# A last expert of at most 64 rows, computed on unsplit fp32 values in two column tiles

## The chip, the cores and the metric

The kernel runs on one core of a Trainium2 chip. The metric is device microseconds of one execution. Three executions of the kernel before took 591.93, 593.94 and 595.46 us (median 593.94). A fourth, taken by the hardware profiler, took 592.76 us; its trace spans 591.0 us.

## The reference

Linear attention gives the rows `x`, and a layer of eight experts works on them, each row by the one expert that its gate picks:

```python
q_s = softmax(q, axis=-1); k_s = softmax(k, axis=2)      # q, k, v: 8 x 8 x 576 x 64
x = q_s @ (k_s.T @ v)                                    # as 4608 rows of 512
logits = x @ w_gate; expert_idx = argmax(logits, axis=1)
gate_w = softmax(logits)[arange(N), expert_idx]
for e in range(8):                                       # w1[e]: 512 x 1024, w2[e]: 1024 x 512
    h = maximum(x_sorted[lo:hi] @ w1[e], 0.0)
    y_sorted[lo:hi] = h @ w2[e]
return gate_w[:, None] * y_sorted[inv_perm]
```

How many rows each expert gets is known only once the gates are computed. For the inputs of this case the reference gives 1150, 0, 542, 34, 595, 578, 0 and 1709 rows to experts 0 to 7.

## The kernel before

The first part (to about 148 us) is the attention. It writes each row of `x`, with its gate and its row number, into a scratch area in DRAM (`xs`) at a place of its expert. Then `tables` counts the rows of each expert, and `t5`, a chain of tiny VectorE operations on 8 partitions, works out a table `tab`: which experts have rows, in which order they come (expert 0, then by falling count), in how many steps, and how many tiles of 128 rows each step has. The chain ends in a matmul (`t6`) that brings the fields onto one partition, and `t8` writes them to `tab`, from which every engine reads registers.

The second part (`experts`) is a loop of steps. Each engine has its own program (`pe`, `act`, `dve`, `pool`, `sp`) and they meet at semaphores only. ACT, DVE and POOL run one `body` per step (14 here), PE one `pe_expert` per expert. A step works on up to three tiles, `W` = 384 rows. Its products are made from split values: every fp32 number is kept as a rounded high part and the low rest (`XH`, `XL`, `W1H`, `W1L`, `HH`, `HL`, `W2H`, `W2L`), and each product is three matmuls (high by high, low by high, high by low).

- `layer1(w)` on PE makes the hidden values transposed: for each of 8 blocks of 128 hidden units, 12 matmuls (3 products by 4 blocks of the inner dimension) with `w` columns. From block 5 on it waits until DVE has read an earlier block out of the same PSUM bank (`sHL[PREV[f]]`).
- ACT (`relus`) applies relu to each block into `HH`, DVE (`lows`) makes `HL` from it. In the first step of an expert ACT and DVE also split `w2` into `W2H` and `W2L`.
- `layer2(u)` makes one tile's output: 24 matmuls of 512 columns into `PY[u]`.
- ACT (`yout`) scales a tile by its gate into `YT[u]`, and POOL (`send`) scatters its rows to `out` by an indirect DMA; rows that pad a tile carry a row number out of bounds and are skipped.
- For the step that comes next, DVE (`flip`) turns the loaded rows `XB` into `XX`, ACT and DVE split that into `XH`/`XL`, and, where the next step begins another expert, they split `RAW1` (its `w1`) into `W1H`/`W1L`. SP loads rows two steps ahead (`bload`) and weights one expert ahead (`wload`).

On PE a step of one or two tiles goes through `pe_small`: `layer1` with 256 columns, then one tile, and a second one where the table says so. The last expert here has 34 rows, so its one step is `layer1(256)` and one `layer2`. Which steps ran can be counted in the trace: the 39 evictions `yt<-py` are 9 + 14 + 5 + 5 + 5 + 1 tiles.

What a step costs on PE is set by no planner: the order is that of the code, and the other engines run beside PE as the semaphores let them.

Of the kernel before, what the change touches and what calls it, by code (L numbers as in the profile page):

```python
# [16 lines left out]
P = 128  # L17
# [40 lines left out]
Q = 32  # L58
PE, DVE, ACTE, POOL, SP = "pe", "dve", "act", "pool", "sp"
# [41 lines left out]
def attention_moe(ctx: ExitStack, tc: tile.TileContext, q, k, v, w_gate, w1, w2, xs, out):  # L101
# [661 lines left out]
    def tables():  # L763
# [3 lines left out]
        base, start, steps, total, cnt, tiles, threes, rank, own = [  # L767
            small(name, [E, 1]) for name in ("base", "start", "steps", "total", "cnt", "tiles", "threes", "rank", "mykey")]
# [29 lines left out]
        MADE = 35  # L798

        def t5(sem):  # L800
# [41 lines left out]
            op('F2', 'at end on', lambda: STT(part(fld, 2), at, end, on, op0=ALU.is_equal, op1=ALU.mult))  # L842
            op('V1', 'steps', lambda: TS(V[:, 1:2], steps, 0.0, None, op0=ALU.is_gt))
# [5 lines left out]
            op('total', 'every', lambda: RED(total, every, op=ALU.add, axis=AX.X))  # L849
# [105 lines left out]
def experts(nc, tc, g):  # L955
# [21 lines left out]
    sSp, sSp2 = sem("ssp"), sem("ssp2")  # L977
    sH1, sW1, sW2 = [sem(x, NQ) for x in ("sh1", "sw1", "sw2")]
# [25 lines left out]
    def pe():  # L1004
# [71 lines left out]
        n, i = x.reg("n", 0), x.reg("i", 0)  # L1076

        def again(name, done=1):
            if done:
                x.add("it", 1)  # L1080
            x.add("n", 1)
            e.br_lt(n, E, "pe_expert", name)
            at(name)
            e.br("pe_done")

        e.br("pe_expert")
        with nc.body("pe_expert", valid_engines=[e.engine]):
# [5 lines left out]
            small = x.get(SMALL, r, 0, 2)  # L1093
# [17 lines left out]
            at("pe_small")  # L1111
            step(2 * P, 1)
# [21 lines left out]
    def act():  # L1134
# [30 lines left out]

        def body(j):
            kind = x.get(KD, j, 0, 3)
# [37 lines left out]
    def dve():  # L1205
# [24 lines left out]

        def body(j):
            fresh = x.get(LW, j, 0, 1)
# [39 lines left out]
        e.memset(g.EP[:, :, 1], 0.0).then_inc(sB, 1)  # L1272
        v = lambda t: t.rearrange("p c (u t) -> p u c t", t=P)
# [6 lines left out]
    def pool():  # L1280
# [16 lines left out]

        def body(j):
            kind = x.get(KD, j, 0, 3)
            e.drain()  # L1300
            hold(sGS, it)
# [20 lines left out]
    def sp():  # L1322
# [6 lines left out]
        def xload(j):  # L1329
            n = x.get(KD, j, 0, 3)  # L1330
# [7 lines left out]
        def bload(j):  # L1338
            n = x.get(KD, j, 0, 3)
# [87 lines left out]
```

## Time and profile before

| | |
|---|---|
| three executions | 591.93, 593.94, 595.46 us |
| the profiled execution | 592.76 us |
| its span, first to last instruction | 591.0 us |
| PE busy | 561.2 us, 95% of the span |
| DVE, ACT, POOL busy | 327.9, 254.4, 149.2 us |
| PE in the steps, 200 to 550 us | busy in all of it but 0.14 us |
| last step's first matmul, last matmul, last eviction, end | 567.99, 584.74, 585.16, 591.0 us |

The page gives shares over the whole span. The change concerns its last 23 us and 4 us of the table chain, so those stretches are read in order of time. In rows of the timeline the first number is the start in us, the second the time from the first instruction's start to the last one's end, then engine, line and operation; xN joins N instructions, and what stands in brackets is idle time before and who ended it. "PEq", "SPq" are the engines' instruction queues. In the names of tiles `pt`, `ph` and `py` are PSUM tiles of layer 1 and layer 2, `hid` holds `HH` and `HL`, `raw` holds `RAW1` or `RAW2`.

An fp32 matmul that isn't a transpose shows as two records (pairs of weight load and matmul): the program has 320 matmuls at L374 and the trace 640 records, 32 at L514 and 64. The split products (fp32r) show as one record each.

### The profile page before, as it was taken

The page shows a single profiled execution, that of the slowest core. Times are in us where ns is not written, and L with a number is a line of the kernel's source. Part 1 is how long each engine was busy: PE and PEld are TensorE (multiplying, and loading weights), DVE is VectorE, ACT ScalarE, POOL GpSimd, SP SyncE. Part 2 cuts the span into 40 slices and gives each one's busy share as a digit, 9 for nine tenths or more (in the row PEclk, how much of TensorE's full clock was granted, in tenths as well). Part 3 has the DMA queues.
Part 4 walks back from the last instruction along what each step waited for, and adds up shares of the span by engine and source line. Part 5 has one row for each costly group of instructions (what it writes and reads, how often), then busy time and mean ns, then how long its engine had stood idle before and what let it go on. Part 6 is the DMA issues. An engine that isn't in the chain of part 4 may idle for free.

```text
span 591.0 us, 11678 instructions
## 1 busy us (share of the span) xinstructions
PE 561.2 (95%) x3932; PEld 500.1 (85%) x3933; DVE 327.9 (55%) x644; ACT 254.4 (43%) x514; POOL 149.2 (25%) x243
## 2 busy tenths in 40 slices
PE   6589899989999999999999999999999999999996
PEld 2478778968788989898998989988898989899895
DVE  5899799997663332736141324364626543573644
ACT  1599768865322312433131213253424524262543
POOL 4234759778612010110101010111002010201110
PEclk9699899999999999999999999999999999999999
DMA  8999999855459730074204020305520670153010
GB/s 265 324 346 281 317 321 314 300 183 176 185 189 285 209 90 18 18 231 157 73 0 107 0 71 19 90 0 175 205 72 19 207 229 2 53 192 137 0 40 5
DMA packets 64720, 87.21 MB, mean 148 GB/s; under 512 B 8623, under 2 KB 50095, under 8 KB 64048
## 3 DMA queue, kind: packets, MB, share of 16 engines
q1 hardware_dynamic: 58112, 66.70, 36.3%
q0 software_dynamic: 6000, 19.03, 8.4%
q10 hardware_dynamic: 576, 1.07, 0.5%
q8 instruction: 19, 0.31, 0.2%
q14 instruction: 13, 0.11, 0.1%
HBM read 64.82 MB, written 22.74 MB: 148 GB/s over the span
## 4 chain that ended last, share of the span: by engine, by line
PE 81%; DVE 9%; DMA 3%; ACT 2%; issue 2%; POOL 1%; SPq 0%; POOLq 0%; ACTq 0%; DVEq 0%
PE py L1040 33%; PE pt L1024 17%; PE ph L1024 17%; PE xp L511 3%; PE py L1059 3%; DVE kt L349 2%; DVE qm L442 2%; PE qT L493 2%; PE kv L374 2%; DMA vs<-in_v 1%; PE ph L739 1%; DVE kp L315 1%; DVE xr L526 1%; DMA kt<-in_k 1%; DVE pe L584 1%
## 5 line engine op out<-in xcount | busy, mean ns | idle before, releaser
L1040 PE MATMUL py<-w2h,hid 128*128 128x512 f32 x576 | 179.8, 389 | 0.0
L1040 PEld LDWEIGHTS py<-w2h,hid 128*128 128x128 f32 x576 | 108.2, 188 | 22.1
L1292 POOL DMA_INDIRECT out<-yt,ix x39 | 43.6, 1118 | 313.3 <-ACT yt L1145 313.3
L1040 PE MATMUL py<-w2l,hid 128*128 128x512 f32 x288 | 112.2, 390 | 0.0
L1224 DVE SCALAR_TENSOR_TENSOR hid<-pt,hid 128x384 fp32r<-128x384 f32 x56 | 31.1, 557 | 146.0 <-ACT hid L1154 138.0
L1145 ACT ACTIVATE yt<-py,ga 128x512 f32<-128x512 f32 x39 | 26.8, 688 | 142.1 <-PE py L1040 133.9
L1040 PEld LDWEIGHTS py<-w2l,hid 128*128 128x128 f32 x288 | 54.1, 188 | 10.8
L1224 DVE SCALAR_TENSOR_TENSOR hid<-ph,hid 128x384 fp32r<-128x384 f32 x56 | 31.2, 558 | 55.2 <-ACT hid L1154 55.2
L1154 ACT ACTIVATE hid<-ph 128x384 fp32r<-128x384 f32 x56 | 27.5, 492 | 62.0 <-PE ph L1024 62.0
L1154 ACT ACTIVATE hid<-pt 128x384 fp32r<-128x384 f32 x56 | 27.5, 491 | 61.8 <-PE pt L1024 48.8
L511 PE MATMUL xp<-kx,qTs 128*128 128x146 f32 x256 | 44.3, 316 | 0.8 <-ACT qTs L488 0.7
L1213 DVE STREAM_TRANSPOSE xx<-xb 128x1536 f32<-128x1536 f32 x14 | 40.6, 2902 | 7.3 <-DVE gs L1220 5.0
L1024 PE MATMUL pt<-xh,w1h 128*128 128x384 f32 (+3 forms) x224 | 42.6, 312 | 0.1
L1024 PE MATMUL ph<-xh,w1h 128*128 128x384 f32 (+3 forms) x224 | 42.4, 311 | 0.0
L1024 PE MATMUL pt<-xl,w1h 128*128 128x384 f32 (+3 forms) x224 | 42.4, 311 | 0.0
L1024 PE MATMUL pt<-xh,w1l 128*128 128x384 f32 (+3 forms) x224 | 42.4, 311 | 0.0
L1024 PE MATMUL ph<-xh,w1l 128*128 128x384 f32 (+3 forms) x224 | 42.4, 311 | 0.0
L1024 PE MATMUL ph<-xl,w1h 128*128 128x384 f32 (+3 forms) x224 | 42.4, 311 | 0.0
L631 POOL DMA_INDIRECT xs<-xr,posi x36 | 37.9, 1052 | 15.0 <-issue 13.5
L511 PEld LDWEIGHTS xp<-kx,qTs 128*128 128x128 f32 x256 | 36.8, 198 | 2.8 <-ACT qTs L488 1.1
L1024 PEld LDWEIGHTS pt<-xh,w1h 128*128 128x128 f32 x224 | 35.9, 189 | 1.9 <-issue 0.9
L1024 PEld LDWEIGHTS pt<-xl,w1h 128*128 128x128 f32 x224 | 35.7, 189 | 0.0
(231 smaller groups left out, 931.5 us busy)
## 6 DMA issues: line engine op xcount, KB each, us to landing
raw<-in_moe_w SPq DMA_DIRECT2D x10, 2048.0 KB, 8.2
kt<-in_k SPq DMA_DIRECT2D x14, 640.0 KB
xb<-xs SPq DMA_DIRECT2D x32, 192.0 KB
qt<-in_q SPq DMA_DIRECT2D x8, 640.0 KB
vs<-in_v SPq DMA_DIRECT2D x8, 640.0 KB
qt<-in_q SPq DMA_DIRECT2D x8, 512.0 KB
vs<-in_v SPq DMA_DIRECT2D x8, 512.0 KB
xt<-in_moe_w SPq DMA_DIRECT2D x8, 256.0 KB
```

Source lines behind the costliest of these rows:

```text
L349: TT(t, t, m[:, :, None, :].to_broadcast([P, 2, SLOT, D]), op=ALU.subtract)
L374: nc.tensor.matmul(o.kv[i * D:(i + 1) * D, c, lo:lo + D + 1], o.kt[:, 2 * c + i, j, :], VT[b % 2][:, 2 * c + i, at:at + D + 1], start=Fals ...
L511: nc.tensor.matmul(xv[:, c, :KW], o.qT[i][:, c, :], kx[:, c, :], **flags)
L631: s = nc.gpsimd.indirect_dma_start(out=xs, out_offset=bass.IndirectOffsetOnAxis(ap=n.pi[:, t - t0:t - t0 + 1], axis=0), in_=xr[:, t, :], i ...
L1024: m = e.matmul(ph, wt[:, c, f * P:(f + 1) * P], xt[:, c, :w], start=(n == 0), stop=(n == 3 * NC - 1))
L1040: m = e.matmul(g.PY[u], ht[:, f, u * P:(u + 1) * P], wt[:, f, :], start=(n == 0), stop=(n == 3 * NF - 1))
L1059: m = e.matmul(g.PY[u], ht[:, f, u * P:(u + 1) * P], wt[:, f, :], start=(n == 0), stop=(n == 3 * NF - 1))
L1145: m = e.activation(g.YT[u], g.PY[u], AF.Copy, scale=g.GA[:, u:u + 1]).wait_op(sPY[u], cu[u], GE)
L1154: e.activation(g.HH[:, f, :], g.PH[f][:, :W], AF.Relu).wait_op(sPH[f], it, GE).then_inc(sHH[f], 1)
L1213: e.transpose(g.XX, g.XB.rearrange("p t (a c) -> p c t a", c=NC)).wait_op(sB, b80, GE)
L1224: e.scalar_tensor_tensor(g.HL[:, f, :], g.PH[f][:, :W], 0.0, g.HH[:, f, :].bitcast(F32), op0=ALU.max, op1=ALU.subtract).wait_op(sHH[f], it ...
L1292: e.indirect_dma_start(out=g.out, out_offset=bass.IndirectOffsetOnAxis(ap=g.IX[:, u:u + 1], axis=0), in_=g.YT[u], in_offset=None, bounds_c ...
```

## The change

If the last expert in the order has at most 64 rows and isn't the first one, its only step takes another way (`slim`) on every engine.

- Table: `t5` gets six more operations for `ends`, `few` and `tiny` and for adding them to `V2` and `F0`, with the sum `total` made earlier, so the count `MADE` goes from 35 to 41. For such an expert `KD` is 4 and `SMALL` 4.
- PE: `pe_small` jumps to `pe_slim`. Layer 1 has the rows as the stationary operand (64 columns of it) and `RAW1` as the moving one, 256 columns at a time, unsplit. The two halves of the hidden units (s = 0, 1) go to the two column tiles of 64, whose outputs are PSUM partitions 0 to 63 and 64 to 127. There are two quarters (k = 0, 1) of 8 matmuls each. Then four transposes of 128x128 turn the hidden values, and layer 2 has 16 matmuls of 256 columns, again in two column tiles (d = 0, 1: halves of the output row), into one bank.
- Between them ACT applies relu to quarter 0 and copies its transposes, and DVE does the same for quarter 1.
- ACT evicts one tile of 128x256 scaled by the gate. POOL scatters it as half rows, with row numbers that DVE made from `XD`. SP loads `XD` (two copies of the 64 gates and row numbers) beside the rows.
- In that step nothing is split (`HL`, `W2H`, `W2L`), nothing is flipped, and `XH`/`XL` aren't made. The step before still splits `w1` for it.
- On ACT, DVE, POOL and SP each `body` (and `bload`) first reads `KD` and has a branch more; on PE `again` adds to one more register.

```diff
+SLIM = 64
-        MADE = 35
+        MADE = 41
+            op('total', 'every', lambda: RED(total, every, op=ALU.add, axis=AX.X))
+            op('ends', 'start total', lambda: STT(ends, start, 1.0, total, op0=ALU.add, op1=ALU.is_equal))
+            op('few', 'cnt ends', lambda: STT(few, cnt, float(SLIM), ends, op0=ALU.is_le, op1=ALU.mult))
+            op('tiny', 'few start', lambda: TS(tiny, start, 0.0, 3.0, op0=ALU.is_gt, op1=ALU.mult))
+            op('tiny', 'few', lambda: TT(tiny, tiny, few, op=ALU.mult))
+            op('V2', 'tiny', lambda: TT(V[:, 2:3], V[:, 2:3], tiny, op=ALU.add))
-            op('total', 'every', lambda: RED(total, every, op=ALU.add, axis=AX.X))
+            op('F0', 'on tiny', lambda: STT(part(fld, 0), on, tiny, part(fld, 0), op0=ALU.mult, op1=ALU.add))
...
+        def slim():
+            e.wait_ge(sW1[NQ - 1], it)
+            e.wait_ge(sXL, it)
+            y = g.PH[2]
+            for k in range(2):
+                for c in range(NC):
+                    for s in range(2):
+                        m = e.matmul(g.PH[3 * k][s * SLIM:(s + 1) * SLIM, :256], xx[:, c, :SLIM],
+                                     g.RAW1[:, c, s * 512 + k * 256:s * 512 + (k + 1) * 256], start=(c == 0), stop=(c == NC - 1))
+                m.then_inc(sTH, 1)
+            for k in range(2):
+                e.wait_ge(sTS[k], 1)
+                for i in (2 * k, 2 * k + 1):
+                    m = e.transpose(g.PH[1 + 3 * k][:, i % 2 * P:(i % 2 + 1) * P], g.HS[:, i * P:(i + 1) * P], g.ident)
+                m.then_inc(sTQ, 1)
+            e.wait_ge(sR2, m2)
+            n = 0
+            for k in range(2):
+                e.wait_ge(sTT[k], 1)
+                for i in (2 * k, 2 * k + 1):
+                    for s in range(2):
+                        for d in range(2):
+                            m = e.matmul(y[d * SLIM:(d + 1) * SLIM, :DM // 2], g.HT[:, i * P + s * SLIM:i * P + (s + 1) * SLIM],
+                                         g.RAW2[:, 4 * s + i, d * DM // 2:(d + 1) * DM // 2], start=(n == 0), stop=(n == NF - 1))
+                        n += 1
+            m.then_inc(sTY, 1)
...
+            x.add("m2", 16)
...
+            e.br_cond(small < 3, "pe_short", "pe_slim")
+            at("pe_slim")
+            slim()
+            again("pe_out4")
+            at("pe_short")
             step(2 * P, 1)
...
# act
+        def slim():
+            e.activation(g.HS[:, :256], g.PH[0][:, :256], AF.Relu).wait_op(sTH, 1, GE).then_inc(sTS[0], 1)
+            e.activation(g.HT[:, :256], g.PH[1][:, :256], AF.Copy).wait_op(sTQ, 1, GE).then_inc(sTT[0], 1)
+            e.wait_ge(sTG, 1)
+            e.activation(g.YS, g.PH[2][:, :DM // 2], AF.Copy, scale=g.GD[:, 0:1]).wait_op(sTY, 1, GE).then_inc(sTO, 1)
+            e.sem_inc(sSp2, 1).wait_op(sTZ, 16, GE)
+
         def body(j):
-            kind = x.get(KD, j, 0, 3)
+            kind = x.get(KD, j, 0, 4)
+            with e.If(kind > 3):
+                slim()
+            with e.If(kind < 4):
+                usual(j, kind)
...
# dve
+        def slim():
+            e.sem_inc(sBT, 1)
+            e.wait_ge(sTI2, 3)
+            e.scalar_tensor_tensor(g.ID, g.XD[:, 1:2], 2.0, g.HALVES[:, 1:2], op0=ALU.mult, op1=ALU.add).wait_op(sXD, 32, GE).then_inc(sTI, 1)
+            e.tensor_tensor(g.GD[:, 1:2], g.XD[:, 0:1], g.HALVES[:, 0:1], op=ALU.add).then_inc(sTI, 1)
+            e.reciprocal(g.GD[:, 0:1], g.GD[:, 1:2]).wait_op(sTI, 2, GE).then_inc(sTG, 1)
+            e.tensor_scalar(g.HS[:, 256:], g.PH[3][:, :256], 0.0, None, op0=ALU.max).wait_op(sTH, 2, GE).then_inc(sTS[1], 1)
+            e.tensor_copy(g.HT[:, 256:], g.PH[4][:, :256]).wait_op(sTQ, 2, GE).then_inc(sTT[1], 1)
...
# pool
+        def slim():
+            hold(sTI, 1)
+            hold(sTO, 1)
+            e.indirect_dma_start(out=halves, out_offset=bass.IndirectOffsetOnAxis(ap=g.ID, axis=0), in_=g.YS,
+                                 in_offset=None, bounds_check=2 * N - 1, oob_is_err=False).then_inc(sTZ, 16)
...
# sp, bload
+            with e.If(n > 3):
+                get(1)
+                for s in range(2):
+                    e.dma_start(g.XD[s * SLIM:(s + 1) * SLIM], g.xs[bass.ds(row, SLIM), DM:DM + 2]).then_inc(sXD, 16)
+            with e.If(n < 4):
+                others(n, get)
```

Where the code puts the new work on PE is seen in the order of its instructions. Before, at the start of a step of one or two tiles (L1106 and L1110 are the branches to `pe_some` and `pe_small`):

```order
743 L1110 COMPARE_AND_BRANCH
744 L1024 MATMUL pt<-xh,w1h_61 128x256 x4
745 L1024 MATMUL pt<-xl,w1h_61 128x256 x4
746 L1024 MATMUL pt<-xh,w1l_62 128x256 x4
```

After, PE's new block (L1071 is layer 1, L1077 the transposes, L1086 layer 2) and the branch that leads to it (L1153):

```order
743 L1151 COMPARE_AND_BRANCH
744 L1153 COMPARE_AND_BRANCH
745 L1037 MATMUL pt<-xh,w1h_61 128x256 x4
...
811 L1071 MATMUL pt<-raw_2442,xx 64x256 x8
812 L1071 MATMUL ph_2454<-raw_2442,xx 64x256 x8
813 L1077 MATMUL pt<-ident,hs 128x128 x2
814 L1077 MATMUL ph_2455<-ident,hs 128x128 x2
815 L1086 MATMUL pt<-raw_2151,ht 64x256 x16
```

The old block stays where it was behind one more branch, and 36 matmuls stand 66 rows further on, reached by a jump. Before, DVE's table chain and what follows it, at its end:

```order
356 L846 SCALAR_TENSOR_TENSOR fld<-on,head 8x23
357 L847 TENSOR_TENSOR fld<-row,on 8x23
358 L848 TENSOR_TENSOR fld<-eq,V 8x50
359 L849 TENSOR_REDUCE total<-every 8x1
360 L694 TENSOR_TENSOR w2l_2146<-raw_2148,w2h_2145 128x1024
361 L747 SCALAR_TENSOR_TENSOR hid<-pt,hid 128x384
```

After, the same place on DVE:

```order
362 L853 SCALAR_TENSOR_TENSOR fld<-on,head 8x23
363 L854 TENSOR_TENSOR fld<-row,on 8x23
364 L855 TENSOR_TENSOR fld<-eq,V 8x50
365 L856 SCALAR_TENSOR_TENSOR fld<-on,tiny,fld 8x23
366 L695 TENSOR_TENSOR w2l_2149<-raw_2151,w2h_2148 128x1024
367 L748 SCALAR_TENSOR_TENSOR hid<-pt,hid 128x384
```

`total` has moved up to row 337, a new write of the field `F0` ends the chain, and the split of `w2` behind it comes six rows later.

## Rows read from the trace of the kernel before

**Rows 1.** The page: busy time of the engines (share of the span, instructions).

```profile
PE 561.2 (95%) x3932; PEld 500.1 (85%) x3933; DVE 327.9 (55%) x644; ACT 254.4 (43%) x514; POOL 149.2 (25%) x243
```

**Rows 2.** Busy time by stretch: PE, PEld, DVE, ACT, POOL, granted clock, DMA share, GB/s.

```profile
500.00:550.00 50.00, 50.00 (x297) 45.49 (x296) 27.05 (x37) 20.51 (x35) 6.33 (x7) 1.00 0.32 113
60.00:75.00 15.00, 12.39 (x161) 11.22 (x159) 11.60 (x27) 11.59 (x24) 11.35 (x17) 0.89 0.95 315
```

**Rows 3.** The last step in order of time.

```profile
567.99 0.64 PE L1024 MATMUL pt<-xh,w1h 128*128 128x256 f32 x4
568.19 0.69 ACT L1145 ACTIVATE yt<-py,ga 128x512 f32<-128x512 f32 x1 [4.75 <-PE py L1040]
570.49 0.49 ACT L1154 ACTIVATE hid<-pt 128x384 fp32r<-128x384 f32 x1 [1.61 <-PE pt L1024]
571.01 0.56 DVE L1224 SCALAR_TENSOR_TENSOR hid<-pt,hid 128x384 fp32r<-128x384 f32 x1 [7.97 <-ACT hid L1154]
575.18 0.64 PE L1024 MATMUL pt<-xh,w1h 128*128 128x256 f32 x4
584.74 0.39 PE L1040 MATMUL py<-w2h,hid 128*128 128x512 f32 x1
585.16 0.69 ACT L1145 ACTIVATE yt<-py,ga 128x512 f32<-128x512 f32 x1 [3.08 <-PE py L1040]
586.75 0.98 POOL L1292 DMA_INDIRECT out<-yt,ix  x1 [13.89 <-ACT yt L1145]
```

**Rows 4.** The chain that ended last, 567.5 to 591 us, by line.

```profile
by line: PE py L1040 26.2%; PE ph L1024 24.5%; PE pt L1024 24.5%; POOL out L1292 4.2%; issue 3.2%; ACT yt L1145 3.0%; POOLq L1308 0.2%; POOLq L993 0.2%; POOLq L1292 0.1%; POOLq L1288 0.1%
```

**Rows 5.** Timeline: fp32 in two column tiles (L514, L374), and change of shape.

```profile
139.23 0.18 PE L508 MATMUL xp<-eps,ones 128*128 128x4 bf16 x1
139.33 0.72 PE L514 MATMUL xp<-kx,ql 128*64 128x146 f32 x8
...
62.98 0.80 PE L374 MATMUL kv<-vt,kt 128*64 128x65 f32 x20
```

**Rows 6.** Timeline: fp32 on the whole array (L511), and transposes (L493).

```profile
144.91 0.60 PE L493 MATMUL qT<-ident,qs 128*128 128x128 f32 x4
145.98 0.74 PE L511 MATMUL xp<-kx,qTs 128*128 128x146 f32 x4
```

**Rows 7.** Matmul records of two lines: duration ns min/median/max.

```profile
L514 PE MATMUL xp<-kx,ql x64: 286/289/338, 47.4 to 139.8; 128*64 128x146 f32 x64
L374 PE MATMUL kv<-vt,kt x640: 219/222/370, 24.4 to 127.3; 128*64 128x65 f32 x160
```

**Rows 8.** Groups of 128x256 on ACT and DVE: busy us, mean ns.

```profile
L497 ACT ACTIVATE ql<-qT 128x256 f32<-128x256 f32 x8 | 3.1, 382 | 2.5 <-PE qT L493 2.5
L316 DVE TENSOR_TENSOR km<-kp 128x256 f32<-128x256 f32 x16 | 6.8, 425 | 0.5
```

**Rows 9.** The table chain's end and PE beside it, in order of time.

```profile
165.22 0.14 DVE L830 SCALAR_TENSOR_TENSOR cut<-quarter,big 8x1 f32<-8x1 f32 x1
167.75 0.14 DVE L849 TENSOR_REDUCE total<-every 8x1 f32<-8x8 f32 x1
167.83 1.20 DVE L694 TENSOR_TENSOR w2l<-raw,w2h 128x1024 fp32r<-128x1024 f32 x1
169.91 0.36 PE L855 MATMUL pt<-fld,ones 8*1 8x119 f32 x2
170.50 0.56 DVE L747 SCALAR_TENSOR_TENSOR hid<-pt,hid 128x384 fp32r<-128x384 f32 x1 [1.47 <-ACT hid L744]
```

**Rows 10.** Timeline: a stretch after PE sat idle.

```profile
66.39 0.63 PE L493 MATMUL qT<-ident,qs 128*128 128x128 f32 x4 [2.61 <-DVE kt L349]
67.68 1.32 PE L511 MATMUL xp<-kx,qTs 128*128 128x146 f32 x4
```

**Rows 11.** The page, DMA queues: instruction loads (packets, MB, share).

```profile
q8 instruction: 19, 0.31, 0.2%
```

**Rows 12.** The scatters of L1292, from issue to landing.

```profile
DMA to landing us min/median/max: 2.3/3.4/8.7
```

More of the change, by code (lines that the diff above doesn't have):

```diff
@@ L766, in tables @@
         V = small("V", [E, NFLD])
-        base, start, steps, total, cnt, tiles, threes, rank, own = [
-            small(name, [E, 1]) for name in ("base", "start", "steps", "total", "cnt", "tiles", "threes", "rank", "mykey")]
+        base, start, steps, total, cnt, tiles, threes, rank, own, ends, few, tiny = [
+            small(name, [E, 1]) for name in ("base", "start", "steps", "total", "cnt", "tiles", "threes", "rank", "mykey", "ends", "few", "tiny")]
         key = small("key", [E, E])
@@ L942, in attention_moe @@
         I0.XG, I0.GN, I0.EP = [bx.tile([P, 3, 2], F32, name=n) for n in ("xg", "gn", "ep")]
+        I0.HS, I0.HT = [bx.tile([P, 512], F32, name=n) for n in ("hs", "ht")]
+        I0.YS = bx.tile([P, DM // 2], F32, name="ys")
+        I0.XD, I0.GD, I0.HALVES = [bx.tile([P, 2], F32, name=n) for n in ("xd", "gd", "halves")]
+        I0.ID = bx.tile([P, 1], I32, name="id")
         PT = qs.tile([P, 3, NC, P], F32, name="pt")
@@ L977, in experts @@
     sSp, sSp2 = sem("ssp"), sem("ssp2")
+    sTH, sTQ, sTY, sTO, sTI, sTG, sXD, sTI2, sTZ = [sem(x) for x in ("sth", "stq", "sty", "sto", "sti", "stg", "sxd", "sti2", "stz")]
+    sTS, sTT = [sem(x, 2) for x in ("sts", "stt")]
     sH1, sW1, sW2 = [sem(x, NQ) for x in ("sh1", "sw1", "sw2")]
@@ L1092, in pe @@
             rest = x.get(REST, r, 0, 5)
-            small = x.get(SMALL, r, 0, 2)
+            small = x.get(SMALL, r, 0, 4)
             e.reg_mov(i, 0)
@@ L1229, in lows, with usual @@
                         m.then_inc(sW2[f // 2], 1)
-        def body(j):
+        def slim():
[6 more added lines that the diff above has]
+            e.tensor_copy(g.HT[:, 256:], g.PH[4][:, :256]).wait_op(sTQ, 2, GE).then_inc(sTT[1], 1)
+        def body(j):
+            kind = x.get(KD, j, 0, 4)
+            with e.If(kind > 3):
+                slim()
+            with e.If(kind < 4):
+                usual(j)
+        def usual(j):
             fresh = x.get(LW, j, 0, 1)
@@ L1272, in dve @@
         e.memset(g.EP[:, :, 1], 0.0).then_inc(sB, 1)
+        e.memset(g.HALVES[:, 0:1], EPS).then_inc(sTI2, 1)
+        for s in range(2):
+            e.memset(g.HALVES[s * SLIM:(s + 1) * SLIM, 1:2], float(s)).then_inc(sTI2, 1)
         v = lambda t: t.rearrange("p c (u t) -> p u c t", t=P)
@@ L1296, in send, with usual @@
                 x.add(f"d{u}", 16)
+        halves = g.out.rearrange("n (s d) -> (n s) d", s=2)
+        def slim():
[3 more added lines that the diff above has]
+                                 in_offset=None, bounds_check=2 * N - 1, oob_is_err=False).then_inc(sTZ, 16)
         def body(j):
-            kind = x.get(KD, j, 0, 3)
+            kind = x.get(KD, j, 0, 4)
             e.drain()
+            with e.If(kind > 3):
+                slim()
+            with e.If(kind < 4):
+                usual(kind)
+        def usual(kind):
             hold(sGS, it)
@@ L1329, in xload @@
         def xload(j):
-            n = x.get(KD, j, 0, 3)
+            n = x.get(KD, j, 0, 4)
             row = x.get(ROW, j, 0, E * RS)
@@ L1338, in bload @@
         def bload(j):
-            n = x.get(KD, j, 0, 3)
+            n = x.get(KD, j, 0, 4)
             row = x.get(ROW, j, 0, E * RS)
@@ L1347, in get, with others @@
                 e.dma_start(g.XG[:, :m], rows[:, DM:DM + 2].rearrange("(u p) w -> p u w", p=P)).then_inc(sB, 16)
+            with e.If(n > 3):
+                get(1)
+                for s in range(2):
+                    e.dma_start(g.XD[s * SLIM:(s + 1) * SLIM], g.xs[bass.ds(row, SLIM), DM:DM + 2]).then_inc(sXD, 16)
+            with e.If(n < 4):
+                others(n, get)
+        def others(n, get):
             with e.If(n > 2):
```

3 lines of the change are left out of this document (2 added, 1 removed).

## The prediction

> **What bounds the kernel now.** I read the page first: PE is busy for 95% of the span [rows 1]. The stretches in the expert steps say the same more sharply, 50.00 of 50 us at full clock, while DVE and ACT are busy for about half of it [rows 2]. So work taken from DVE or ACT there is worth nothing, and work taken from PE is worth all its time as long as nothing takes its place. Then the chain of waits over the last 23 us: three quarters of it are the two layers on PE, and behind them stand only one eviction, one scatter and their hand-offs [rows 4]. The timeline puts times to it [rows 3]: the last expert's first matmul starts at 567.99, its last one ends at 584.74 + 0.39 = 585.13, the eviction starts at 585.16, the scatter at 586.75, and the span ends at 591.0. PE thus spends 17.14 us on 34 rows, and from the eviction's end (585.85) to the end of the span another 5.15 us go by.
>
> **What is removed.** All of these 17.14 us: 96 matmuls of 256 columns and 24 of 512. The splits of `w2` and of the hidden values in this step, and one flip, go too; they lay beside PE (the first low part ends at 571.57 and PE needs it at 575.18 [rows 3]) and count as nothing. The split of `w1` for this expert stays, in the step before, beside PE as ever.
>
> **What the matmuls cost.** The new layers have 16 + 16 matmuls of 256 columns in unsplit fp32, and such a matmul makes two records, so 32 + 32 records. The trace has this form already: fp32, 128 rows deep, in turns on two column tiles. Eight records of 146 columns take 0.72 us, the last one 0.289 of that, so one follows another after (0.72 - 0.289)/7 = 0.062 us [rows 5, 7], 0.42 ns a column. Twenty of 65 columns: (0.80 - 0.222)/19 = 0.030 us, 0.47 ns a column. On the whole array, four records of 146 columns need (0.74 - 0.289)/3 = 0.150 us each, 1.03 ns a column [rows 6]. For 256 columns the bounds are 0.108 us (nearest in width), 0.120 us, and 0.263 us if two tiles gave nothing. I take 0.108: 32 x 0.108 = 3.46 us for each layer.
>
> Between a matmul of the whole array and one in column tiles 0.10 us pass from start to start [rows 5], and I charge 0.1 us at each of three such changes. [...]
>
> **The new chain,** in us after 567.99:
> - 0.1 to 3.56: layer 1. Its last record ends 0.18 later (0.289 - 0.108), at 3.74. Quarter 0 is done near 2.0, and ACT has its relu ready long before PE is free. ACT's own lead-in allows that: in the step of before it began its first relu 1.61 us after the previous eviction, at 2.5 here, with three table reads before it [rows 3]; now it is one read.
> - DVE takes quarter 1 from 3.77 to 4.20. An operation of 128x256 is 0.425 us on DVE and 0.382 us on ACT [rows 8].
> - PE transposes quarter 0 from 3.66 to about 4.06 (four transposes take 0.60 us [rows 6], two about 0.40), and ACT's copy is done at 4.47. PE transposes quarter 1 from 4.23 to 4.63, and DVE's copy is done at 5.09, inside the first half of layer 2. Here PE stands idle for the only time, twice 0.1 to 0.2 us.
> - 4.6 to 8.06: layer 2, its last record ending at 8.24. The eviction starts at 8.27, where it was 585.16 - 567.99 = 17.17. That is 8.90 us earlier.
> - The eviction is 128x256 with a scale: between 0.382 us [rows 8] and the 0.69 us of twice the size [rows 3]. I take 0.42, 0.27 less than before.
> - POOL waits for the eviction and scatters 128 partitions, as now. It is one instruction of 0.98 us [rows 3], as before, so the 5.15 us stay. Half rows make 68 writes of 1 KB where 34 of 2 KB were; I cost that at nothing, and at 0.5 us either way for the range.
>
> Sum: 8.90 + 0.27 = 9.2 us less.
>
> **What is added elsewhere.** Six operations in the table chain: from L830 at 165.22 to L849 at 167.75 there are 19 steps of 0.133 us, so 0.8 us. The chain ended at 167.89, and PE's `t6` waits for it behind layer 1 until 169.91: 2.0 us of cover, 1.2 of them left. The split behind the chain now ends at 169.83 rather than 169.03, and DVE's next operation waits for ACT until 170.50 anyway [rows 9]. Nothing. If each of the six took 0.33 us, the cover would be gone and PE would wait for the rest. Three memsets of 128 values or fewer come behind, before a wait of DVE; nothing. SP issues two small loads of 64 gates and row numbers beside the rows, two steps ahead; behind them on SP's queue stand only weights that are wanted a step later. On DVE the wait for these loads (`sXD`) has the relu of quarter 1 queued behind it, but they land some 20 us earlier; nothing. ACT's wait for the gate (`sTG`) stands before the eviction, and DVE makes the gate before layer 1 is through.
>
> Each step's `body` gets one branch more, and on DVE and ACT a table read in another place. PE sees it only if the first low part comes late; 575.18 - 571.57 = 3.6 us of cover each step [rows 3]. Nothing.
>
> **The time.** The profiled execution was 592.76 us, 1.76 more than its span, and lies 1.18 below the median of the three runs. By it the changed kernel takes 583.6 us, by the median 584.7; against the mean of all four, 593.5, it is 584.3, which I forecast.
>
> **Rivals.**
> - *Code that has never run.* PE jumps to a block 66 rows on, and ACT, DVE and POOL enter blocks for the first time at the moment that decides. If one load of code fell on the chain, it would cost about the shortest landing of a scatter, 2.3 us [rows 12], two of them 4.6: 586.6 to 588.9 us. For: instructions are loaded in pieces during the run [rows 11]. Against: PE came into its last step without a gap [rows 3], and ACT, DVE and POOL arrive early. 10%.
> - *Two tiles overlap only in part.* Two streams of fp32 are read at once, for longer than in any row. Half way between 0.108 and 0.263 us is 0.186: 64 x 0.078 = 5.0 us more, 589.3 us. Against it: rows 5 at two widths, which agree within 11%. 4%. [...]
> - *No overlap at all at this width*: 64 x 0.155 = 9.9 us more, 594.2 us, no change. 3%.
> - [...] After PE had been idle for 2.61 us, four records of L511 took 1.32 us instead of 0.74, in a stretch with a granted clock of 0.89 [rows 2, 6, 10]. If the gaps between the layers did that at once, both layers and the transposes would take 7.4 us more: 591.7 us, within 0.5%. Against: here no gap is over 0.3 us. 3%.
> - *Slower: the added branch makes every step load code anew.* The place is the beginning of each `body` on ACT and DVE, which now jumps over a block. It decides from 3.6 us a step, where the first low part reaches PE too late. Two loads of 2.3 us a step would be 1.0 us past that, over 13 steps 13 us: 584.3 + 13 = 597 us. Against: 19 loads in the whole span, for all engines and 14 steps [rows 11]. 2%.
> - *The way isn't taken*, because the last expert has more rows than 64 or the fields come out otherwise. The routing gives it 34 rows, and the trace shows a last step of one tile. Then nothing changes but the chain: 593.5 us. 1%.
>
> **How the numbers follow.** The forecast has 77%; its own range is 582.2 to 586.5 (the lowest run, 591.93, less 9.7, to the sum with 0.120 us a record, dearer changes of shape and a slow run). The code rival takes it to 588.0, which leaves out the rest. A change of 0.5%, 3 us, is about what can be told from none here. Faster by more: 77 + 10 + 4 = 91%. Within it: 3 + 3 + 1 = 7%. Slower: 2%.
>
> **What would show it.** In the new trace: a pitch of 0.11 us in 32 records of 256 columns in each layer; the eviction about 8.3 us after layer 1 begins; no gap of PE over 0.3 us in between; 5.1 us from eviction to end; PE's `t6` following layer 1 without a wait; the steps from 200 to 550 us as long as before. A pitch of 0.2 or more, or PE waiting over a microsecond for a relu or a copy, makes the sum wrong.

## The result and the profile after

The changed kernel takes 585.65 us (median of 4 runs, 583.73 to 588.12) against 593.84 us (4 runs, 591.93 to 595.46). The ratio is 0.9857, with an interval of 0.983 to 0.9884; by it 8.5 us less (6.9 to 10.1), where the two medians differ by 8.2. Run again on another chip it was 585.08 us against 594.2, a ratio of 0.9842 (0.9817 to 0.9868). The profiled execution took 583.73 us with a span of 581.9 (592.76 and 591.0 before). In the trace the last instruction ends at 581.95, before at 590.99.

The page after; columns as in [rows 1], and below it the queue that loads instructions:

```profile
PE 552.1 (95%) x3880; PEld 489.2 (84%) x3881; DVE 314.7 (54%) x637; ACT 245.0 (42%) x498; POOL 149.8 (26%) x242
...
q8 instruction: 19, 0.31, 0.2%
```

PE lost 9.1 us of busy time (561.2 - 552.1) and its share stayed at 95%. That is how a cut on the bounding engine looks: the span fell by as much. The instruction loads are 19, as many as in [rows 11]. A stretch of the steps in between, columns as in [rows 2]:

```profile
500.00:550.00 50.00, 50.00 (x299) 45.42 (x298) 26.96 (x37) 20.06 (x36) 6.56 (x7) 1.00 0.32 113
```

PE has no gap in it, as in the first line of [rows 2], and it is busy for all of the 350 us from 200 to 550 (349.86 before). What the branch added to each step costs is measured in e2 below. The last step in order of time, which answers to [rows 3]:

```profile
567.09 0.39 PE L1053 MATMUL py<-w2h,hid 128*128 128x512 f32 x1
567.41 1.95 PE L1071 MATMUL pt<-raw,xx 128*64 128x256 f32 x16
...
569.18 1.90 PE L1071 MATMUL ph<-raw,xx 128*64 128x256 f32 x16
569.40 0.38 ACT L1213 ACTIVATE hs<-pt 128x256 f32<-128x256 f32 x1 [1.20 <-PE pt L1071]
...
571.01 0.44 PE L1077 MATMUL pt<-ident,hs 128*128 128x128 f32 x2
571.13 0.42 DVE L1296 TENSOR_SCALAR hs<-ph 128x256 f32<-128x256 f32 x1 [11.27 <-PE ph L1071]
571.48 0.39 ACT L1214 ACTIVATE ht<-pt 128x256 f32<-128x256 f32 x1 [1.70 <-PE pt L1077]
...
571.61 0.44 PE L1077 MATMUL ph<-ident,hs 128*128 128x128 f32 x2 [0.16 <-DVE hs L1296]
...
572.01 3.67 PE L1086 MATMUL pt<-raw,ht 128*64 128x256 f32 x32
572.08 0.42 DVE L1297 COPY ht<-ph 128x256 f32<-128x256 f32 x1 [0.53 <-PE ph L1077]
575.73 0.47 ACT L1216 ACTIVATE ys<-pt,gd 128x256 f32<-128x256 f32 x1 [3.86 <-PE pt L1086]
577.09 0.97 POOL L1381 DMA_INDIRECT out<-ys,id  x1 [7.04 <-ACT ys L1216]
```

L1071 is layer 1 (two quarters of 16 records), L1077 the transposes, L1086 layer 2: the new way was taken. PE waits for another engine once, for 0.16 us. The eviction starts 575.73 - 567.41 = 8.32 us after the layers begin, where it was 17.17. The records of layer 1's first quarter (duration ns min/median/max, first and last start):

```profile
L1071 PE MATMUL pt<-raw,xx x16: 379/379/430, 567.4 to 569.0; 128*64 128x256 f32 x16
```

A group of sixteen in column tiles takes 1.95 us from first start to last end. With 0.379 for the last, one follows another after (1.95 - 0.379)/15 = 0.105 us on the mean. Record by record the trace has them start in pairs, one in each tile, and a pair every 0.216 us; the two of a pair start 0.006 us apart in layer 1 and 0.036 us apart in layer 2.

What follows the eviction, with the same columns:

```profile
L1217 ACTq EVENT_SEMAPHORE  x1: 17/17/17, 579.3 to 579.3; - x1
...
L1262 ACTq EVENT_SEMAPHORE  x3: 17/17/17, 579.8 to 579.9; - x3
...
L1125 PEldq COMPARE_BRANCH  x1: 169/169/169, 580.0 to 580.0; - x1
```

L1217 is ACT's wait for the scatter: it passes at 579.3, 2.2 us after the scatter began. ACT then returns to its loop, and its last waits (L1262) pass at 579.9. PE, after its last matmul, still reads the table for the experts without rows, and leaves its loop with the branch at L1125, 3.8 us after the eviction's end (576.20). From there to the end at 581.95 go 5.75 us, where 5.13 went before (5.15 with the rounded span).

The end of the table chain and PE beside it, as in [rows 9]:

```profile
167.66 0.22 DVE L856 SCALAR_TENSOR_TENSOR fld<-on,tiny,fld 8x23 f32<-8x23 f32 x1
167.81 1.21 DVE L695 TENSOR_TENSOR w2l<-raw,w2h 128x1024 fp32r<-128x1024 f32 x1
...
168.85 0.86 PE L740 MATMUL ph<-xh,w1l 128*128 128x384 f32 x4
...
169.64 0.36 PE L862 MATMUL pt<-fld,ones 8*1 8x119 f32 x2
```

The chain ends at 167.88. `t6` (L862) still follows layer 1 (L740) without a wait.

### The profile page after: what moved, and what is told of

Same layout as the page of the kernel before. It is cut to its first block, busy times and chain, and to the rows that moved or that the text cites. A ratio compares the mean times of both kernels' runs of the same rounds, so it can differ in the third digit from the quotient of the medians.

```text
span 581.9 us, 11673 instructions
## 1 busy us (share of the span) xinstructions
PE 552.1 (95%) x3880; PEld 489.2 (84%) x3881; DVE 314.7 (54%) x637; ACT 245.0 (42%) x498; POOL 149.8 (26%) x242
## 4 chain that ended last, share of the span: by engine, by line
PE 81%; DVE 7%; DMA 4%; ACT 2%; issue 2%; POOL 1%; SPq 1%; POOLq 0%; ACTq 0%; DVEq 0%
PE py L1053 33%; PE pt L1037 16%; PE ph L1037 16%; PE xp L512 3%; DMA vs<-in_v 3%; PE py L1099 3%; PE kv L375 2%; DVE kt L350 2%; PE qT L494 2%; PE ph L740 1%; DVE qm L443 1%; DMA kt<-in_k 1%; DVE xr L527 1%; DVE pe L585 1%; ACT vt L178 1%
## 5 line engine op out<-in xcount | busy, mean ns | idle before, releaser
L1053 PE MATMUL py<-w2h,hid 128*128 128x512 f32 x560 | 174.7, 389 | 0.0
L1053 PEld LDWEIGHTS py<-w2h,hid 128*128 128x128 f32 x560 | 105.1, 188 | 21.6
L1053 PE MATMUL py<-w2l,hid 128*128 128x512 f32 x280 | 109.1, 390 | 0.0
L1272 DVE STREAM_TRANSPOSE xx<-xb 128x1536 f32<-128x1536 f32 x13 | 37.8, 2906 | 18.2 <-issue 18.2
L1037 PE MATMUL pt<-xh,w1h 128*128 128x384 f32 (+3 forms) x208 | 39.9, 313 | 0.0
L1037 PE MATMUL ph<-xl,w1h 128*128 128x384 f32 (+3 forms) x208 | 39.8, 313 | 0.0
L1037 PE MATMUL pt<-xl,w1h 128*128 128x384 f32 (+3 forms) x208 | 39.8, 313 | 0.0
L1037 PE MATMUL ph<-xh,w1h 128*128 128x384 f32 (+3 forms) x208 | 39.8, 313 | 0.0
L1037 PE MATMUL ph<-xh,w1l 128*128 128x384 f32 (+3 forms) x208 | 39.8, 313 | 0.0
L1037 PE MATMUL pt<-xh,w1l 128*128 128x384 f32 (+3 forms) x208 | 39.8, 313 | 0.0
L1037 PEld LDWEIGHTS pt<-xh,w1h 128*128 128x128 f32 x208 | 33.6, 189 | 1.4 <-issue 0.6
L1037 PEld LDWEIGHTS ph<-xh,w1h 128*128 128x128 f32 x208 | 33.4, 189 | 0.0
```

Of the source, the lines that this page charges most:

```text
L1037: m = e.matmul(ph, wt[:, c, f * P:(f + 1) * P], xt[:, c, :w], start=(n == 0), stop=(n == 3 * NC - 1))
L1053: m = e.matmul(g.PY[u], ht[:, f, u * P:(u + 1) * P], wt[:, f, :], start=(n == 0), stop=(n == 3 * NF - 1))
L1272: e.transpose(g.XX, g.XB.rearrange("p t (a c) -> p c t a", c=NC)).wait_op(sB, b80, GE)
```

## The experiments

The rows below have the columns of the timeline (start us, duration us, engine, line, operation) where nothing else is said. Where no number of runs is given, the time is that of one execution.

### The same kernel again: a1_again

> The changed kernel once more, beside the kernel before on one chip, for a narrower interval. By its trace it should be 8.5 to 9.2 us faster: ratio 0.983 to 0.987.

Measured: 585.08 us (6 runs, 582.26 to 587.08), ratio 0.9842 (0.9817 to 0.9868). From the first matmul of the new layers to the eviction 8.32 us, from its end to the end of the span 5.80. The way to the eviction repeats to a hundredth of a microsecond. What scatters is when the last step begins: 567.41 and 567.62 in these two profiles, 570.31 in e6 below. That scatter arises before the steps: the first step's first matmul (L1037) starts at 187.92, 188.17 and 190.84, and from it to the new layers go 379.5 us in all three. In e6 the granted clock was 0.76 from 163 to 170 us, where it was 1.00 in the other two.

### The additions without the new way: e2_way_not_taken

```diff
-            op('few', 'cnt ends', lambda: STT(few, cnt, float(SLIM), ends, op0=ALU.is_le, op1=ALU.mult))
+            op('few', 'cnt ends', lambda: STT(few, cnt, -1.0, ends, op0=ALU.is_le, op1=ALU.mult))
```

> The changed kernel with all that it adds (table operations, table reads, branches, code), but with the threshold set so that no expert goes the new way. Theory (all additions are covered): the time of the kernel before, ratio 0.998 to 1.002 and a span of 591 us; the table chain about 0.3 us longer, PE's table matmul still right behind layer 1, PE busy from 200 to 550 us. Rival (the added branches cost in each step): 0.2 us or more in each of 14 steps, ratio 1.005 or more.

Measured: 593.95 us (12 runs) against 593.26 (17 runs), ratio 1.0003 (0.9988 to 1.0018). The six operations, the branches and the longer code cost at most 0.2% together, and the whole gain, within that, comes from the last step. In its profile the last step, computed in the old way, began at 567.52 (567.99 before): the earlier start of the profiled execution after doesn't come from the new way.

### One tile's records ahead of the other's: e1_serial

```diff
-                for c in range(NC):
-                    for s in range(2):
+                for s in range(2):
+                    for c in range(NC):
...
-                for i in (2 * k, 2 * k + 1):
-                    for s in range(2):
-                        for d in range(2):
+                for d in range(2):
+                    for i in (2 * k, 2 * k + 1):
+                        for s in range(2):
...
```

> The changed kernel with the same 32 matmuls, but those of one column tile in a row (all of the first half, then all of the second) in both layers, so that neighbours share a tile. Theory (the two column tiles run side by side, one record needs 0.21 us or more by itself): a pitch of 0.21 to 0.26 us, each layer 6.8 to 8.4 us instead of 3.5, the eviction 15 to 18 us after layer 1 begins instead of 8.3, the span 589 to 592 us. Rival (a record of 256 columns needs 0.11 us whatever its neighbour, and order means nothing): pitch 0.11, eviction at 8.3, span 582 us.

Measured: 587.03 us, the eviction 10.35 us after the layers begin, between the 8.32 of the changed kernel, whose records overlap in pairs, and the 15.18 of e10 below, whose records share one tile, so neither side of the expectation came true. The records of layer 1 and the eviction:

```profile
568.91 2.21 PE L1071 MATMUL pt<-raw,xx 128*64 128x256 f32 x13
...
570.75 0.43 PE L1071 MATMUL ph<-raw,xx 128*64 128x256 f32 x1
...
570.96 0.38 PE L1071 MATMUL pt<-raw,xx 128*64 128x256 f32 x1
...
571.02 0.38 PE L1071 MATMUL ph<-raw,xx 128*64 128x256 f32 x1
...
571.18 0.38 PE L1071 MATMUL pt<-raw,xx 128*64 128x256 f32 x1
...
571.23 0.38 PE L1071 MATMUL ph<-raw,xx 128*64 128x256 f32 x1
...
571.39 0.38 PE L1071 MATMUL pt<-raw,xx 128*64 128x256 f32 x1
...
579.26 0.47 ACT L1214 ACTIVATE ys<-pt,gd 128x256 f32<-128x256 f32 x1 [4.85 <-PE pt L1085]
```

Here `pt` and `ph` are the two quarters; each has eight records in the first column tile and then eight in the second. In the program all sixteen records of `pt` stand ahead of those of `ph`. Yet a record of `ph`, in the first column tile, starts at 570.75, and three of `pt`, in the second, start only at 570.96, 571.18 and 571.39: in this trace a record of one tile passes three of the other that the program has ahead of it. The passing did not reach far enough to overlap all, and the written order is worth 10.35 - 8.32 = 2.0 us here. Why it stops at three the trace doesn't show.

### Both halves in one column tile: e10_one_tile

```diff
...
-                        m = e.matmul(g.PH[3 * k][s * SLIM:(s + 1) * SLIM, :256], xx[:, c, :SLIM],
+                        m = e.matmul(g.PH[3 * k][:SLIM, :256], xx[:, c, :SLIM],
...
-                            m = e.matmul(y[d * SLIM:(d + 1) * SLIM, :DM // 2], g.HT[:, i * P + s * SLIM:i * P + (s + 1) * SLIM],
+                            m = e.matmul(y[:SLIM, :DM // 2], g.HT[:, i * P + s * SLIM:i * P + (s + 1) * SLIM],
...
```

The order of the loops in layer 1 and the flags that start and end a sum are changed to fit; half of the last expert's values are overwritten or left out.

> The changed kernel with both halves of the hidden units, and both halves of the output row, in the first column tile, so that all 64 records share one tile; half of the last expert's values are overwritten or left out by that. Theory (a tile takes 0.216 us for a record, and two run at once): pitch 0.216 throughout, 6.9 us a layer, eviction 15.2 to 15.4 us after layer 1 begins, span about 589 us, still 2 us below the kernel before. Rival (full overlap isn't needed, the engine finds other gaps): eviction at 10 to 11 us, as when the halves were run in turn.

Measured: 592.05 us, the eviction 15.18 us after the layers begin.

```profile
569.12 3.67 PE L1071 MATMUL pt<-raw,xx 128*64 128x256 f32 x16
...
572.62 3.62 PE L1071 MATMUL ph<-raw,xx 128*64 128x256 f32 x16
...
577.17 7.09 PE L1086 MATMUL pt<-raw,ht 128*64 128x256 f32 x32
...
584.30 0.47 ACT L1216 ACTIVATE ys<-pt,gd 128x256 f32<-128x256 f32 x1 [7.28 <-PE pt L1086]
```

With the same number of records of the same shape, sixteen take 3.67 us rather than 1.95: (3.67 - 0.379)/15 = 0.219 us each, twice the 0.105. So the second column tile is worth 15.18 - 8.32 = 6.9 us of the change. Without it the new path would still reach the eviction 2.0 us sooner than the old one with its 17.17.

### Keeping the split, on 64 columns: e3_split_64_columns

```diff
-            op('F0', 'on tiny', lambda: STT(part(fld, 0), on, tiny, part(fld, 0), op0=ALU.mult, op1=ALU.add))
+            op('F0', 'on tiny', lambda: STT(part(fld, 0), on, 0.0, part(fld, 0), op0=ALU.mult, op1=ALU.add))
...
-            slim()
+            step(SLIM, 1)
```

> The last expert goes the old way on split values, only with 64 columns in layer 1 instead of 256. Theory (unsplit values in column tiles are what pays, since with split ones the splits of w2 and of the hidden values on DVE, 0.56 + 0.69 us in each of 8 blocks, become the bound once PE is quick): first relu about 2.4 us in, then 8 blocks at 1.25 us, the eviction 12 to 14 us after layer 1 begins, span 586 to 588 us. Rival (the spared columns are the whole gain): layer 1 at 0.03 to 0.055 us a matmul, 2.9 to 5.3 us, layer 2 5.4 us, eviction at 8.4 to 11 us, span 582 to 585 us.

Measured: 622.88 us, ratio 1.0511 (1.048 to 1.0542), 30 us slower than before. Neither theory had this. Layer 1 first:

```profile
590.30 0.60 PE L1037 MATMUL pt<-xh,w1h 128*128 128x64 f32 x4
...
590.74 0.61 PE L1037 MATMUL pt<-xl,w1h 128*128 128x64 f32 x4
```

Four matmuls of 64 columns take 590.74 - 590.30 = 0.44 us, 0.11 each, where 256 columns took (575.18 - 567.99)/60 = 0.12, five blocks of 12 by [rows 3]. So 64 columns instead of 256 spare 0.01 us a matmul in these rows, and computing fewer rows in the old way would have gained about 96 x 0.01 = 1 us in layer 1, by estimate. Then the 30 us. The page's queue of instruction loads:

```profile
q8 instruction: 37, 0.61, 0.4%
```

and a step's first matmul in the timeline:

```profile
469.43 1.19 PE L1037 MATMUL pt<-xh,w1h 128*128 128x256 f32 x4 [6.44 <-issue]
```

There are 37 instruction loads instead of 19, and PE stands 6.44 us before the first matmul of a step, released by nothing that the trace shows. The step of 64 columns is written out a second time, which makes PE's loop longer. This was a new theory: the length of PE's loop, not what it computes.

### The length of PE's loop alone: e8_code_120, e9_code_60, e11_code_20

The three put a block of 120, 60 or 20 matmuls that no run enters into PE's loop over the experts, behind a branch (60 shown):

```diff
-            small = x.get(SMALL, r, 0, 4)
+            small = x.get(SMALL, r, 0, 5)
...
+            e.br_cond(small < 5, "pe_slim2", "pe_spare")
+            at("pe_spare")
+            for i in range(60):
+                e.matmul(g.PY[0], g.HH[:, i % NF, :P], W2H[:, i % NF, :], start=(i == 0), stop=(i == 60 - 1))
+            again("pe_out5")
+            at("pe_slim2")
             slim()
```

> The changed kernel with a block of 120 more matmuls in PE's loop over the experts that is never entered (the same count as the 64-column step of the earlier experiment, beside the new block instead of in its place). Theory (the size of PE's loop decides whether its code stays loaded): instruction loads on the PE's queue go on after 440 us, branches of PE take 3.5 us and more, PE stands idle for 6 us at the beginning of some steps, the span is 605 us or more. Rival (the 64-column step itself, or its late clock, made the earlier run slow): nothing changes, 582 to 584 us.

> The same with 60 matmuls that are never entered. Theory of a cliff right above the changed kernel's size: as with 120, only fewer loads, 590 us or more. Theory with some room left: 582 to 584 us with no load after 440 us. Rival of the earlier run (not the size): 582 to 584 us here and with 120.

> The same with 20 matmuls that are never entered. With 60 PE's code was loaded anew at step after step and the span was 609 us; the changed kernel itself loads nothing after 440 us. If there is room for 20: 582 to 584 us and no load after 440 us. If the changed kernel stands right at the edge: loads after 440 us, PE idle for 3 us or more at some steps, 590 us or more.

Measured: 614.68 us with 120, 610.87 with 60, 585.06 with 20. The span with 60 is 609.1 us, 27 more than after; with 20 it is 583.3, within the spread, with 19 loads as before. Of the kernel with 60, PE's branches at L1136 (duration ns min/median/max):

```profile
L1136 PEldq COMPARE_BRANCH  x8: 64/204/3779, 186.7 to 603.2; - x8
```

a gap before a step in the timeline:

```profile
466.29 1.20 PE L1037 MATMUL pt<-xh,w1h 128*128 128x256 f32 x4 [6.03 <-issue]
```

PE's waits from 440 us on (us, times, longest):

```profile
PE pt L1037 <- issue: 16.5, 4, 6.2
```

and what followed three of the gaps, columns as in [rows 2]:

```profile
465.00:472.00 7.00, 5.71 (x27) 5.74 (x28) 1.25 (x2) 1.32 (x4) 0.18 (x1) 0.52 0.67 264
...
496.00:502.00 6.00, 5.20 (x18) 5.20 (x19) 0.56 (x1) 0.58 (x2) 0.18 (x1) 0.50 0.21 50
533.00:540.00 7.00, 3.29 (x15) 3.32 (x16) 0.00 (x0) 0.35 (x1) 0.24 (x2) 0.52 0.60 190
```

Branches that take 0.2 us else take up to 3.78, and PE idles 16.5 us in four gaps; 18 of its 37 instruction loads lie in this stretch. Behind three of the gaps, of 3.2 to 6.2 us, the granted clock is 0.50 to 0.52: PE's 5.71 + 5.20 + 3.29 = 14.2 us of busy time there would take some 7 us at full clock, by estimate. At the end the branch that leaves the loop (L1125, 0.17 us else) takes 3.4 us, and from the eviction's end to the span's end go 8.98 us for 5.75. The gaps, the 7 us and these 3.2 make 26.7 of the 27. Shown is that 60 matmuls which never run cost some 25 us here (610.87 for 585.65) and 20 cost nothing (585.06). Where between the two it begins, whether bytes or blocks decide, and whether the place of the block in the loop counts, was not tried.

### Sixty operations more in the table chain: e7_sixty_more

```diff
-        MADE = 41
+        MADE = 101
...
+            for _ in range(60):
+                op('big', 'threes', lambda: TS(big, threes, 1.0, None, op0=ALU.min))
```

> The changed kernel with sixty more tiny operations at the end of the table chain, each repeating an earlier one and changing nothing. They last some 4.0 us (0.067 us each), and the chain of the changed kernel ended 1.76 us before PE's table matmul. Theory (the cover is that and no more): the table matmul waits 2.2 us, the span grows by 2.2 us to 584. Rival (later waits absorb it, or the split behind the chain delays PE once more): a span of 582, or of 586.

Measured: 595.45 us, span 593.7, 11.8 more than after, and more than was expected.

```profile
178.38 0.55 PE L864 MATMUL pt<-fld,ones 8*1 8x119 f32 x2 [7.07 <-DVE big L858]
```

A window behind it, columns as in [rows 2]:

```profile
174.75:185.00 10.25, 6.62 (x16) 4.87 (x17) 8.64 (x38) 0.00 (x0) 0.00 (x0) 0.50 0.00 0
```

The sixty operations write the same tile, each waits for the one before, and they follow at 0.175 us, so they take 10.5 us. PE waits 7.07 us for them; the other 3.4 us lie beside PE's layer 1. On top of it the granted clock is 0.50 from 174.75 to 185 us, though PE works again from 178.38: its 6.62 us there would take 3.3 at full clock, by estimate. It was also 0.76 from 165 to 171 us, for the most part before the sixty began, where the changed kernel has 1.00; that is another 1.5 us, and the three make the 11.8. The size in the expectation was wrong, the cover is real.

### Who holds the end: e4_short_exit and e6_half_the_writes

e4 lets PE leave its loop behind the last expert, and moves the wait for the scatter from ACT to POOL:

```diff
             slim()
-            again("pe_out4")
+            e.br("pe_done")
...
-            e.sem_inc(sSp2, 1).wait_op(sTZ, 16, GE)
...
                                  in_offset=None, bounds_check=2 * N - 1, oob_is_err=False).then_inc(sTZ, 16)
+            hold(sTZ, 16)
```

> The changed kernel, but after the new way PE goes to the end of its program at once, past the experts without rows, and POOL rather than ACT waits for the last scatter to land. From the eviction's end to the end of the span took 5.15 us before and 5.75 us after the change. Theory (the way out of the engines' programs is longer: PE's table reads for empty experts and ACT's return through its loop now end last): 5.1 to 5.3 us. Rival (68 half rows take longer to write than 34 whole ones): 5.7 us as now.

e6 leaves out half of the scatter's writes:

```diff
-            e.memset(g.HALVES[s * SLIM:(s + 1) * SLIM, 1:2], float(s)).then_inc(sTI2, 1)
+            e.memset(g.HALVES[s * SLIM:(s + 1) * SLIM, 1:2], float(1000000 * s)).then_inc(sTI2, 1)
```

> The changed kernel with the row numbers of the second halves out of bounds, so the second half of each output row of the last expert is not written: 34 writes of 1 KB instead of 68. Theory (the end is set by the way out of the programs): from the eviction's end to the end 5.6 to 5.8 us, as with all writes. Rival (the number of writes): 5.1 to 5.3 us.

Measured: 585.67 us with a span of 583.9, and 586.68 with 584.9; both began the last step later than after did (569.81 and 570.31), so the ends are compared and not the times. The eviction of e4:

```profile
578.13 0.47 ACT L1216 ACTIVATE ys<-pt,gd 128x256 f32<-128x256 f32 x1 [3.86 <-PE pt L1086]
```

and that of e6:

```profile
578.63 0.47 ACT L1216 ACTIVATE ys<-pt,gd 128x256 f32<-128x256 f32 x1 [3.86 <-PE pt L1086]
```

From the eviction's end to the last instruction's end: 583.89 - 578.60 = 5.29 us in e4, 584.89 - 579.10 = 5.79 in e6 (5.75 and 5.80 in the two profiles of the changed kernel). Half the writes change nothing; the shorter exit gives back some 0.5 us. The traces of e1 and e10 take ACT's part and PE's part of it apart. Both have the exit of the changed kernel, but their records follow more slowly, and PE leaves its loop sooner after the last one. In e10 PE leaves its loop here:

```profile
L1125 PEldq COMPARE_BRANCH  x1: 169/169/169, 586.8 to 586.8; - x1
```

That is 2.0 us after the eviction's end (584.30 + 0.47) rather than 3.8, and ACT, 3.9 us after it as ever, is the last to finish. From the eviction's end to the last instruction's end go 5.49 us in e10 and 5.48 in e1. So PE's late exit is worth 0.3 us, and ACT's turn through its loop, which e4 takes away too, the other 0.2.

### Transposes among the matmuls: e5_woven

With the exit of e4, it puts quarter 0's transposes into the middle of quarter 1 of layer 1, and quarter 1's into the first half of layer 2:

```diff
...
+            one(0, range(NC)).then_inc(sTH, 1)
+            one(1, (0, 1))
+            turn(0)
+            one(1, (2, 3)).then_inc(sTH, 1)
...
+            two(0)
+            turn(1)
+            two(1)
```

> The short exit, and PE's new block woven: the transposes of quarter 0 stand in the middle of layer 1's quarter 1, and those of quarter 1 in the middle of the first half of layer 2. Theory (what is left between the layers is waits for relu and copy, some 0.45 us that can be filled): eviction 7.8 to 8.0 us after layer 1 begins, span about 581 us, ratio to the kernel before 0.983. Rival (each change of shape costs 0.1 us or more, and there are four more of them): eviction at 8.3 us or later.

Measured: 584.25 us (5 runs), ratio 0.983 (0.9813 to 0.9847): faster than the kernel before, not shown to be faster than the changed one, whose interval overlaps.

```profile
570.39 1.03 PE L1072 MATMUL ph<-raw,xx 128*64 128x256 f32 x8
...
571.36 0.44 PE L1079 MATMUL pt<-ident,hs 128*128 128x128 f32 x2
...
571.73 1.08 PE L1072 MATMUL ph<-raw,xx 128*64 128x256 f32 x8
...
576.83 0.47 ACT L1228 ACTIVATE ys<-pt,gd 128x256 f32<-128x256 f32 x1 [4.61 <-PE pt L1085]
```

PE no longer waits, but it changes its shape more often, and the eviction comes 576.83 - 568.62 = 8.21 us after the start, 0.11 sooner, between the 7.8 to 8.0 of the theory and the 8.3 of the rival. The end is 5.29 us, as in e4.

## Why the prediction was right, and where its sizes were off

- **The bound.** Right. 9.1 us of PE's work went and the span fell as much, while e2, with all of the additions and the old last step, stands at 1.0003.
- **The two layers.** The term that carried the sum was 0.108 us a record; measured are 0.105 us on the mean of a group. Layer 1 took 3.67 us and layer 2 3.67, last record's end included (forecast 3.64 each). Counted from where the old path's first matmul would have stood, 567.09 + 0.23, the eviction came after 8.41 us rather than 8.27. Of the 0.14, some 0.05 are the two layers, 0.07 the changes of shape and the transposes between them (571.08 to 572.01, 0.93 for the forecast 0.86), and 0.02 the hand-off to ACT. So this step gave 17.17 - 8.41 = 8.76 us of the forecast 8.90. The dearer changes of shape in the forecast's range are a term that no run shows: the change ahead of layer 1 took 567.41 - 567.32 = 0.09 us, and the other two are in the 0.93.
- **The eviction.** 0.47 us rather than 0.42, so 0.22 less than before instead of 0.27.
- **The step that failed in size: "so the 5.15 us stay".** They became 5.75 (from 5.13, unrounded). The scatter itself was what the prediction said, and e6 shows that its writes don't matter. Looked at was POOL's instruction alone; the engines' way out of their programs behind it was not. Before, PE left its loop 2.7 us after the eviction's end (585.85), and ACT's last waits came after that, where the scatter landed:

```profile
L1084 PEldq COMPARE_BRANCH  x1: 172/172/172, 588.6 to 588.6; - x1
...
L1203 ACTq EVENT_SEMAPHORE  x3: 17/17/17, 589.1 to 589.3; - x3
```

Now ACT goes round its loop once more behind its wait, and PE, whose last work is half as long, leaves its loop only 3.8 us after the eviction's end. With both cut away (e4) the end is 5.29 us; PE's share is 0.3 us and ACT's 0.2 (e1, e10). The last 0.1 to 0.2 between 5.13 and 5.29 stays open. The range had 0.5 us for the half rows, which is not where it went.
- **The sum.** 8.76 + 0.22 - 0.62 = 8.4 us. That is 585.1 from the mean of 593.5, beside the two medians of 585.65 and 585.08. The 0.8 us between this and the forecast are the 0.62 of the end, 0.14 and 0.05; all three go one way, and nothing made up for them. The span of the one profiled execution shows 9.0 (590.99 - 581.95) because its last step began 0.67 us earlier. Of that, 0.23 us lie before the first step (188.15 before, 187.92 after) and 0.44 in the steps. e2, without the new way, has the steps as short (from 188.22 to 567.52). Whether the additions shorten them or the one profile of before ran long isn't shown; over e2's 12 runs they gain nothing that can be told.
- **The table chain.** Forecast was 0.8 us more. It ran from 163.39 to 167.88, 4.49 us, before from 163.67 to 167.89, 4.22: 0.27 more. The operation behind a new one starts 0.07 us after it, not 0.133, and one wait in the chain got 0.15 us shorter. Covered, as said; e7 shows what is paid past the cover.
- **Code that has never run.** It cost nothing in this kernel: 19 loads, and the new block begins 0.09 us after the place of the old one.
- **Two tiles overlap in part, or not at all.** Refuted by the pairs, 0.006 and 0.036 us apart, and by a record every 0.105 us. The price named for no overlap was too high: it came from the whole array, and in one column tile e10 has a record every 0.219 us and not 0.263, hence 6.9 us and not 9.9. For the same reason the pitches of 0.150 us on the whole array and 0.062 us in two tiles [rows 5, 6], a factor of 2.4, mix two things: the second tile gave 0.219/0.105 = 2.1 here (e10), and the rest comes with the narrower shape, by an estimate from 1.03 ns a column on the whole array [rows 6] and 0.219/256, or 0.86 ns, in one tile.
- **Slower, by code loaded anew.** It did not happen here; in e9 something like it did, in another place. Not with the bodies of ACT and DVE but with 60 matmuls more in PE's loop there are 37 instruction loads, and the time is 610.87 us, more than the 597 named. The 19 loads were the right evidence that it had not happened.
- **The clock falls.** Not in the last step: the granted clock is 1.00 from 567.4 to 576 us, and PE's longest wait there is 0.16 us. It was 0.50 to 0.52 behind waits of 3.2 to 7.1 us in e7 and e9. In the kernel before it was 0.50 from 67.68 to 69.00 us, where the four records that took 1.32 us stand (1.32 - 0.449)/3 = 0.290 us apart, against 0.150 [rows 6].

## What to carry to other kernels

When one engine is busy throughout, price a rewrite of its last stage by the pitch of its records in the shape that will run, found in rows of the same form; here that came out within 0.14 us of 8.9. Then follow every engine's program to its end, since what was hidden under the last work can stand bare once that work is short (0.6 us here). Code that never runs wasn't free on this engine, 25 us for 60 matmuls (e9) and nothing for 20 (e11): count the instruction loads before and after.

## What was not expected of the hardware

- Records of two column tiles start 0.006 us apart in layer 1 and 0.036 in layer 2, and each tile keeps a record every 0.216 us, at 256 columns of fp32; in e1 a record of one tile starts ahead of three of the other that the program has before it.
- With 60 matmuls in PE's loop that never run, 18 of the 37 instruction loads come after 440 us, PE stands idle for up to 6.2 us at a time, and the time is 25 us longer (e9). With 20 there are 19 loads, and nothing is lost (e11).
- In e3 the granted clock fell to 0.50 with PE never idle, in the stretch of 64-column matmuls. Two windows of e3, columns as in [rows 2]:

```profile
590.30:595.20 4.90, 4.90 (x45) 4.90 (x45) 1.67 (x4) 2.93 (x7) 1.02 (x2) 1.00 0.04 13
595.20:608.00 12.80, 12.80 (x58) 12.51 (x58) 7.42 (x14) 6.22 (x13) 0.69 (x1) 0.50 0.00 0
```

PE is busy for all of both windows by the trace, and the clock stands at 1.00 in the first and at 0.50 in the second. The layers of the new path kept 1.00 to their end (567.4 to 576 us).
